# A fused attention and two-MLP kernel: other tiles for the second MLP's split activations and w_out sums, another DMA queue for weight stores, later result stores

## The chip, the cores and the metric

The kernel runs on one core of one Trainium2 chip. The metric is the device time of one execution in microseconds (us), median of several runs. The engines named here are TensorE (PE, with its weight loads PEld), VectorE (DVE), ScalarE (ACT), GpSimd (POOL) and SyncE (SP). SP computes nothing here: it issues DMAs, in order, one instruction after the other. ACT and POOL can issue DMAs too.

## The reference

Attention of 8 batches, 8 heads, 512 tokens and 32 state rows gives 4352 rows of 512. Two MLPs follow, each 512 to 2048 to 512 wide. Cut to what matters:

```python
x = attention(x, state)                     # 4352 x 512
h = x @ w_in                                # first MLP, 512 -> 2048
g = np.where(h >= 1, h, np.where(h <= -1, 0, (h + 1) ** 2 / 4))
x = g @ w_out                               # 2048 -> 512
h = x @ moe2_w_in                           # second MLP, 512 -> 2048
g = np.maximum(h, 0) + alpha * np.minimum(h, 0)
out = g @ moe2_w_out                        # 2048 -> 512, 4352 x 512
```

All inputs and outputs are fp32.

## The kernel before

**Precision.** Every fp32 operand of a product is split into a high and a low part (`hi_`, line 73, a cast on ACT; `lo_`, line 76, a subtraction on DVE, for some on POOL), and a product is three matmuls: high times high, high times low, low times high.

**Phases.** Up to about 730 us the kernel does attention and the first MLP. Beside them it prepares the second MLP's weights: sums of weight blocks, split into high and low, are stored to DRAM in `w1c` (from w_in) and `w2c` (from w_out) by `w_store` (line 681 on), and w_out in another order to `wod` by `w2o_store`. A part of the w2c sums is made in the first 50 or so items of the second MLP (`later` in `second`). In the first MLP POOL loads the split weights `ws` (line 489) from its own queue; these loads wait for nothing but their place in POOL's order and a free tile.

**The second MLP** (`second`, from about 728 us to the end) does both products by a Strassen form of seven products instead of eight. Tokens are worked on in five groups s = 0 to 4, of half-widths w = 512, 512, 384, 384, 384. There are 280 *h items* (`h_item`: one w_in product p of one block q, 6 matmuls of 128x128 by 128xw) and 280 *o items* (`o_item`: one quarter jj of a w_out product p, also 6 matmuls). An h item takes its weights from a tile `w1_qp` that `w1_get` loads (256 KB, SP); an o item takes them from `w2` tiles, where before one load of 512 KB serves two items (`w2_load`). The two kinds alternate: h item k+36 stands beside o item k.

After an h item its sum in PSUM goes through `h_after`: ACT copies it out or runs the slope, DVE adds on. For an o item, `o_prep` (three items ahead) makes the operand and splits it into `gh` (ACT) and `gl` (DVE). The products p = 0, 5, 6, 3 of the o items go one after the other into the same two PSUM tiles `oA`, and after each product (four items) `o_after` copies the state of the sum out: `c<-o`, by ACT on a group's first row r (line 836), by a DVE addition on its second (line 838). The next product of the chain adds on in the same PSUM tile, so its first matmul (`o<-gh`, line 824) has to wait for that copy.

On a group's second row the results are turned by DVE (`o_turn`, `ot`) for the products 3, 4, 2, 1 and stored by `ld.dma_start` in line 863: SP issues 64 KB DMAs, 16 or 12 in a row, twice for each group s.

**Tiles.** `U` gives one of 80 tiles of 2 KB a partition, `V` one of 11 of 4 KB. Before, w1, gh, gl, g, c and xh/xl are U tiles; w2 pairs, xr and ot are V tiles.

**Order.** The functions are called in program order; a list scheduler then goes through these instructions with modelled times and fixes the order on every engine and which slot a tile takes. On the chip each engine works in that order. A DMA that SP issues stands still until its destination tile is free, and everything behind it on SP with it.

In names such as `w1_213` the digits are q = 21 and p = 3; in `w2_450` r = 4, p = 5, jj = 0; `gh124` and `gs124` belong to o item 124; `c2110` is group 2, hh 1, tk 1, cc 0.

Of the kernel before, what the change touches and what calls it, by code (L numbers as in the profile page):

```python
# [9 lines left out]
F32 = mybir.dt.float32  # L10
F32R = mybir.dt.float32r
# [29 lines left out]
def kernel_body(ctx: ExitStack, tc: tile.TileContext, x, state, w1i, w1o, w2i, w2o, alpha, out):  # L41
# [52 lines left out]
    vd = [[dp.tile([NH, 128, 512], F32, name=f"vd{g}_{k}") for k in range(4)] for g in range(2)]  # L94
    xd = dp.tile([NO, 128, TOK], F32, name="xd")
    w1c = dp.tile([8, 7, 128, 512], F32, name="w1c")
    w2c = dp.tile([7, 4, 128, 1024], F32, name="w2c")
    wod = dp.tile([NF, 128, 512], F32, name="wod")
    wd = [dp.tile([2, DM, 512], F32, name=f"wd{k}") for k in range(4)]
    GRP = [1, 4]  # L100
# [581 lines left out]
    def w_store(key, *products):  # L682
        for p in products:
            t = WS.pop((key, p)).bitcast(F32)
            j = key[1]
            dst = w1c[j, p] if key[0] == "i" else w2c[p, j // 2, :, j % 2 * 512:(j % 2 + 1) * 512]
            ld.dma_start(out=dst, in_=t)

    def w2o_store(f):
        ld.dma_start(out=wod[f], in_=G.pop(("dec", ("w2o", f))))  # L690


    NSUP = len(HALF)

    BASE = [2 * sum(HALF[:s]) for s in (0, 1, 2, 4, 3)]
    C0 = [BASE[s // 2] + (s % 2) * HALF[s // 2] for s in range(2 * NSUP)]
    XR, XB, XT, HB, GB, GS, OA, OC, OT = {}, {}, {}, {}, {}, {}, {}, {}, {}

    def wof(s):
        return HALF[s]  # L700
# [42 lines left out]
            W1[q, p] = t  # L743

    def w2_load(m):
        if m < len(L2) and m % 2 == 0:
            r, p, jj = L2[m]
            t = V(f"w2_{r}{p}{jj}", F32R)
            ld.dma_start(out=t.bitcast(F32), in_=w2c[p, r % 2 * 2 + jj // 2])
            W2[m], W2[m + 1] = t[:, :512], t[:, 512:]  # L750

    def h_item(q, p):
        s = q // 8
# [38 lines left out]
    def o_prep(m):  # L792
        if m >= len(L2):
            return
        r, p, jj = L2[m]
        s = r // 2
        w, q = wof(s), 4 * r + jj
        b11, b21, b12, b22 = [GB[q, e, tk] for tk in range(2) for e in range(2)]
        src = {0: b11, 5: b11, 6: b12, 4: b11, 2: b22, 1: b21}.get(p)
        if p == 5:  # L800
            dve.tensor_tensor(out=b12, in0=b22, in1=b12, op=ALU.subtract)
            dve.tensor_tensor(out=b11, in0=b12, in1=b11, op=ALU.add)
        elif p == 3:
            src = U(f"t4{q}")[:, :w]
            dve.tensor_tensor(out=src, in0=b21, in1=b11, op=ALU.subtract)
        elif p == 4:
            dve.tensor_tensor(out=b11, in0=b22, in1=b11, op=ALU.subtract)
        h, l = U(f"gh{m}", F32R)[:, :w], U(f"gl{m}", F32R)[:, :w]
        hi_(h, src)
        lo_(l, src, h)  # L810
        GS[m] = (h, l)
# [17 lines left out]
    def o_after(r, p, cc, ps):  # L829
        s, last = r // 2, r % 2  # L830
        w = wof(s)
        hh, tk = {0: (0, 0), 5: (0, 1), 6: (1, 1), 3: (1, 0), 4: (1, 1), 2: (0, 1), 1: (0, 0)}[p]
        key = s, hh, tk, cc
        if p in A_CHAIN and not last:
            OC[key] = U(f"c{s}{hh}{tk}{cc}")[:, :w]
            act.copy(OC[key], ps)  # L836
        else:
            dve.tensor_tensor(out=OC[key], in0=ps, in1=OC[key], op=ALU.add)  # L838
        if last and p in (3, 4, 2, 1):
            o_turn(s, hh, tk, cc, OC.pop(key))  # L840

    def o_turn(s, hh, tk, cc, c):
        w, k = wof(s), 2 * hh + cc
        for v in range(0, w, 256):
            n = min(256, w - v)
            if (s, tk, v) not in OT:
                OT[s, tk, v] = [V(f"ot{s}{tk}{v}"), 0]
            o = OT[s, tk, v][0]
            dve.transpose(out=o[:, :4 * n].rearrange("p (j k x) -> p k j x", k=4, x=32)[:, k],
                          in_=c[:, v:v + n].rearrange("p (j t) -> p j t", t=32))  # L850
            OT[s, tk, v][1] += 1
            if OT[s, tk, v][1] < 4:
                continue
            del OT[s, tk, v]
            for u in range(0, n, 128):
                b, qq = divmod((C0[2 * s + tk] + v + u) // 128, 4)
                for i in range(4):
                    if b < NB:
                        dst = out[b * ROWS:b * ROWS + S, :].rearrange("(j t r) c -> t j r c", t=32, r=4)[:, :, qq]
                    else:  # L860
                        dst = out.rearrange("(b r) c -> r b c", r=ROWS)[S:, 4 * qq:4 * qq + 4]
                    eng = (ld, act)[i % 2] if s == NSUP - 1 else ld
                    eng.dma_start(out=dst[:, :, i * 128:(i + 1) * 128],
                                  in_=o[32 * i:32 * i + 32, 4 * u:4 * u + 512].rearrange("p (j c) -> p j c", j=4))

    def second():


        LAG = 36.5
        ev = [(n, 0, n) for n in range(len(L1))] + [(LAG + m, 1, m) for m in range(len(L2))]  # L870
# [8 lines left out]
        for _, kind, n in sorted(ev):  # L879
            if kind == 0:  # L880
                u, k, q, p = L1[n]
                h_item(q, p)
                h_after(q, p)
                w1_get(n + AW)
                todo = later.pop(n, [])
                s, j = divmod(u, 8)
                if j >= 6 and s + 1 < NSUP:
# [13 lines left out]
                run(*todo)  # L901
            else:
                if n == 0:
                    for m in range(6):
                        w2_load(m)
                    o_prep(0)
                    o_prep(1)
                    o_prep(2)
                w2_load(n + 6)
                o_prep(n + 3)  # L910
                o_item(n)


    side = defaultdict(list)
# [108 lines left out]
        at(gi(8, 2 + 2 * k), x_prep, 0, p)  # L1023
    for k, m in ((1, 3), (3, 2), (7, 4), (9, 1)):
        at(gi(8, k), x_sums, 0, m)
    AW = 7
    for k in range(AW):
        at(gi(8, 7 + k), w1_get, k)
    for j in range(2):
# [91 lines left out]
```

## Time and profile before

| what | value |
|---|---|
| median of 3 runs | 1438.97 us (1438.78 to 1440.12) |
| profiled execution, its own time | 1441.02 us |
| its span in the profile | 1439.1 us |
| PE busy | 1375.6 us, 96% of the span |
| DVE, ACT, POOL busy | 77%, 57%, 6% |
| DMA traffic | 320.62 MB, mean 223 GB/s |
| chain that ended last | PE 82%, DMA 9%, DVE 4%, ACT 2%, issue 2% |

The table is read so: an engine that is busy for 96% of the span leaves 63.5 us in which it did nothing; the waits and the timeline show where. A span is what the profiler saw from the first instruction to the last; the run's own time is 1.92 us longer. Matmul durations on PE overlap by their pipelining; an h or o item of 6 matmuls takes 1.36 us at w = 512 and 1.04 us at w = 384 at full clock (2.4 GHz; the other level is 1.2 GHz).

### The profile page before, as it was taken

The page shows a single profiled execution, that of the slowest core. Times are in us where ns is not written, and L with a number is a line of the kernel's source. Part 1 is how long each engine was busy: PE and PEld are TensorE (multiplying, and loading weights), DVE is VectorE, ACT ScalarE, POOL GpSimd, SP SyncE. Part 2 cuts the span into 40 slices and gives each one's busy share as a digit, 9 for nine tenths or more (in the row PEclk, how much of TensorE's full clock was granted, in tenths as well). Part 3 has the DMA queues.
Part 4 walks back from the last instruction along what each step waited for, and adds up shares of the span by engine and source line. Part 5 has one row for each costly group of instructions (what it writes and reads, how often), then busy time and mean ns, then how long its engine had stood idle before and what let it go on. Part 6 is the DMA issues. An engine that isn't in the chain of part 4 may idle for free.

```text
span 1439.1 us, 20152 instructions
## 1 busy us (share of the span) xinstructions
PE 1375.6 (96%) x6596; PEld 1168.0 (81%) x6596; DVE 1112.0 (77%) x2089; ACT 825.1 (57%) x1658; POOL 90.7 (6%) x94
## 2 busy tenths in 40 slices
PE   6799999999999999999999799999999899899997
PEld 4466688887787888888987678878888899799997
DVE  7888685868788997764858787868786877687687
ACT  5566676777776867664755464435444544364452
POOL 1000001111100000000200020001000100010000
PEclk9999999999999999999999999999999999999999
DMA  6898316788946543353859984676766876885773
GB/s 208 308 320 292 118 51 160 206 250 248 278 175 199 198 163 131 104 181 132 308 197 391 357 273 149 197 228 242 237 206 207 298 236 224 317 304 174 256 296 89
DMA packets 201111, 320.62 MB, mean 223 GB/s; under 512 B 53296, under 2 KB 82992, under 8 KB 201008
## 3 DMA queue, kind: packets, MB, share of 16 engines
q1 hardware_dynamic: 160288, 301.01, 61.4%
q0 software_dynamic: 33280, 8.51, 3.2%
q10 hardware_dynamic: 7440, 9.83, 2.0%
q8 instruction: 52, 0.85, 0.3%
q14 instruction: 51, 0.42, 0.1%
HBM read 242.10 MB, written 76.55 MB: 221 GB/s over the span
## 4 chain that ended last, share of the span: by engine, by line
PE 82%; DMA 9%; DVE 4%; ACT 2%; issue 2%; SPq 0%; ACTq 0%; POOL 0%; DVEq 0%; POOLq 0%
PE o L824 21%; PE accA L614 19%; PE ha L766 12%; PE hA L84 11%; PE hb L766 6%; PE accA L606 3%; PE hc L766 3%; DMA w<-w1c 2%; PE vgp L84 1%; DMA x<-in_x_dram 1%; DMA ws<-wd 1%; PE sc L84 1%; PE sr L84 1%; DMA vr<-vd 1%; DMA wr_wi<-in_moe_w_in_dram 1%
## 5 line engine op out<-in xcount | busy, mean ns | idle before, releaser
L824 PE MATMUL o<-gh,w 128*128 128x384 f32 (+1 forms) x1120 | 350.6, 363 | 19.4 <-ACT c L836 17.9
L76 DVE TENSOR_TENSOR gl<-g,gh 128x512 fp32r<-128x512 f32 (+2 forms) x368 | 234.3, 643 | 32.0 <-ACT gh L73 30.3
L824 PEld LDWEIGHTS o<-gh,w 128*128 128x128 f32 x1120 | 210.7, 191 | 39.6 <-ACT c L836 19.2
L73 ACT CAST gh<-g 128x512 fp32r<-128x512 f32 (+2 forms) x368 | 205.4, 565 | 36.2 <-DVE g L582 27.4
L824 PE MATMUL o<-gl,w 128*128 128x384 f32 (+1 forms) x560 | 203.0, 362 | 3.6 <-DVE gl L76 3.6
L766 PE MATMUL ha<-xh,w 128*128 128x384 f32 (+1 forms) x640 | 202.1, 358 | 1.0 <-ACT g L785 1.0
L773 ACT ACTIVATE m<-g 128x384 f32<-128x384 f32 (+1 forms) x120 | 68.3, 569 | 129.9 <-DVE g L789 127.9
L582 DVE SCALAR_TENSOR_TENSOR g<-y,hA 128x512 f32<-128x512 f32 (+1 forms) x144 | 93.9, 652 | 58.5 <-ACT y L580 58.0
L766 PEld LDWEIGHTS ha<-xh,w 128*128 128x128 f32 x640 | 119.4, 189 | 14.5 <-ACT g L785 3.5
L579 ACT ACTIVATE y<-hA 128x512 f32<-128x512 f32 (+1 forms) x144 | 82.5, 573 | 69.2 <-PE hA L84 67.5
L785 ACT COPY g<-ha 128x384 f32<-128x384 f32 (+1 forms) x120 | 62.9, 524 | 96.7 <-PE ha L766 93.8
L824 PEld LDWEIGHTS o<-gl,w 128*128 128x128 f32 x560 | 107.0, 191 | 12.6 <-DVE gl L76 5.0
L766 PE MATMUL ha<-xl,w 128*128 128x384 f32 (+1 forms) x320 | 114.2, 357 | 0.0
L766 PE MATMUL hb<-xh,w 128*128 128x384 f32 (+1 forms) x320 | 102.3, 360 | 6.2 <-DVE g L789 6.2
L789 DVE TENSOR_TENSOR g<-hb,g 128x384 f32<-128x384 f32 (+1 forms) x80 | 48.7, 609 | 66.9 <-PE hb L766 56.9
L774 DVE SCALAR_TENSOR_TENSOR g<-m,beta_sb,g 128x384 f32<-128x384 f32 (+1 forms) x120 | 81.4, 679 | 22.1 <-ACT m L773 20.8
L580 ACT ACTIVATE y<-y 128x512 f32<-128x512 f32 (+1 forms) x144 | 87.6, 608 | 4.4
L766 PEld LDWEIGHTS hb<-xh,w 128*128 128x128 f32 x320 | 59.5, 188 | 15.1 <-DVE g L789 9.4
L838 DVE TENSOR_TENSOR c<-o,c 128x384 f32<-128x384 f32 (+1 forms) x100 | 59.2, 605 | 12.3 <-PE o L824 11.8
L606 PE MATMUL accA<-g,wf_w1o 128*128 128x512 f32 x128 | 60.8, 607 | 4.6 <-DVE wf_w1o L399 4.6
L766 PEld LDWEIGHTS ha<-xl,w 128*128 128x128 f32 x320 | 60.3, 189 | 5.7
L494 ACT COPY vgo<-vgp 128x512 f32<-128x512 f32 x64 | 37.2, 585 | 41.7 <-PE vgp L84 22.0
(971 smaller groups left out, 3102.2 us busy)
## 6 DMA issues: line engine op xcount, KB each, us to landing
w<-w2c SPq DMA_DIRECT2D x140, 512.0 KB
w<-w1c SPq DMA_DIRECT2D x280, 256.0 KB
vd<-vgo SPq DMA_DIRECT2D x64, 256.0 KB
x<-in_x_dram SPq DMA_DIRECT2D x30, 512.0 KB
vr<-vd SPq DMA_DIRECT2D x56, 256.0 KB
w1c<-wsi SPq DMA_DIRECT2D x56, 256.0 KB
w2c<-wso SPq DMA_DIRECT2D x56, 256.0 KB
wr_wi<-in_moe_w_in_dram SPq DMA_DIRECT2D x16, 512.0 KB
```

Of the source, the lines that this page charges most:

```text
L73: act.copy(h, raw)
L76: (eng or dve).tensor_tensor(out=l, in0=raw, in1=h.bitcast(F32), op=ALU.subtract)
L84: pe.matmul(ps, a, b, start=(k == 0), stop=(k == n - 1))
L579: act.activation(out=y[:, :n], in_=ps, func=AF.Relu, bias=0.5, scale=0.5)
L580: act.activation(out=y[:, :n], in_=y[:, :n], func=AF.Square)
L582: dve.scalar_tensor_tensor(out=g[:, :n], in0=y[:, :n], scalar=1.0, in1=ps, op0=ALU.min, op1=ALU.max)
L606: pe.matmul(ACC[k], w[:, k * 128:(k + 1) * 128], g, start=(f == 0), stop=(f == NF - 1))
L614: pe.matmul(ACC[k][:, :n], a, b, start=(f == 0 and j == 0), stop=(f == NF - 1 and j == 2))
L766: pe.matmul(ps, a[:, kk], b, start=(first and m == 0), stop=(m == 5), skip_group_check=True)
L773: act.activation(out=m, in_=h, func=AF.Relu, scale=-1.0)
L774: dve.scalar_tensor_tensor(out=g, in0=m, scalar=beta_sb[:, f:f + 1], in1=h, op0=ALU.mult, op1=ALU.add)
L824: pe.matmul(ps, a, b, start=(p in (0, 4, 1) and jj == 0 and k == 0), stop=(jj == 3 and k == 2), skip_group_check=True)
```

## The change

Six things are changed in the second MLP and its preparation.

- `w2c` is laid out in single quarters, and each o item has its own load of 256 KB into a U tile, five items ahead, instead of 512 KB for two into a V tile, six ahead.
- The split operand of an o item is one V tile `gs` (high in the first half, low in the second) instead of two U tiles.
- `w_store` and `w2o_store` (128 DMAs) are issued by POOL instead of SP.
- The result stores are taken out of `o_turn` and issued by `o_store` after the o item that follows the one that completed them.
- On a group's second row product 3 is no longer turned on its own but together with product 1, except in the last group.
- w1 loads run 7 items ahead up to item 36 and 5 ahead from 37 on, instead of 7 throughout.

```diff
--- before.py
+++ after.py
@@ -94,7 +94,7 @@
     vd = [[dp.tile([NH, 128, 512], F32, name=f"vd{g}_{k}") for k in range(4)] for g in range(2)]
     xd = dp.tile([NO, 128, TOK], F32, name="xd")
     w1c = dp.tile([8, 7, 128, 512], F32, name="w1c")
-    w2c = dp.tile([7, 4, 128, 1024], F32, name="w2c")
+    w2c = dp.tile([7, 8, 128, 512], F32, name="w2c")
     wod = dp.tile([NF, 128, 512], F32, name="wod")
     wd = [dp.tile([2, DM, 512], F32, name=f"wd{k}") for k in range(4)]
     GRP = [1, 4]
@@ -683,18 +683,17 @@
         for p in products:
             t = WS.pop((key, p)).bitcast(F32)
             j = key[1]
-            dst = w1c[j, p] if key[0] == "i" else w2c[p, j // 2, :, j % 2 * 512:(j % 2 + 1) * 512]
-            ld.dma_start(out=dst, in_=t)
+            pool.dma_start(out=w1c[j, p] if key[0] == "i" else w2c[p, j], in_=t)
 
     def w2o_store(f):
-        ld.dma_start(out=wod[f], in_=G.pop(("dec", ("w2o", f))))
+        pool.dma_start(out=wod[f], in_=G.pop(("dec", ("w2o", f))))
 
 
     NSUP = len(HALF)
 
     BASE = [2 * sum(HALF[:s]) for s in (0, 1, 2, 4, 3)]
     C0 = [BASE[s // 2] + (s % 2) * HALF[s // 2] for s in range(2 * NSUP)]
-    XR, XB, XT, HB, GB, GS, OA, OC, OT = {}, {}, {}, {}, {}, {}, {}, {}, {}
+    XR, XB, XT, HB, GB, GS, OA, OC, OT, DONE = {}, {}, {}, {}, {}, {}, {}, {}, {}, []
 
     def wof(s):
         return HALF[s]
@@ -743,11 +742,10 @@
             W1[q, p] = t
 
     def w2_load(m):
-        if m < len(L2) and m % 2 == 0:
+        if m < len(L2):
             r, p, jj = L2[m]
-            t = V(f"w2_{r}{p}{jj}", F32R)
-            ld.dma_start(out=t.bitcast(F32), in_=w2c[p, r % 2 * 2 + jj // 2])
-            W2[m], W2[m + 1] = t[:, :512], t[:, 512:]
+            W2[m] = U(f"w2_{r}{p}{jj}", F32R)
+            ld.dma_start(out=W2[m].bitcast(F32), in_=w2c[p, r % 2 * 4 + jj])
 
     def h_item(q, p):
         s = q // 8
@@ -805,7 +803,8 @@
             dve.tensor_tensor(out=src, in0=b21, in1=b11, op=ALU.subtract)
         elif p == 4:
             dve.tensor_tensor(out=b11, in0=b22, in1=b11, op=ALU.subtract)
-        h, l = U(f"gh{m}", F32R)[:, :w], U(f"gl{m}", F32R)[:, :w]
+        v = V(f"gs{m}", F32R)
+        h, l = v[:, :w], v[:, 512:512 + w]
         hi_(h, src)
         lo_(l, src, h)
         GS[m] = (h, l)
@@ -836,7 +835,9 @@
             act.copy(OC[key], ps)
         else:
             dve.tensor_tensor(out=OC[key], in0=ps, in1=OC[key], op=ALU.add)
-        if last and p in (3, 4, 2, 1):
+        if last and (p in (4, 2, 1) or p == 3 and s == NSUP - 1):
+            if p == 1 and s < NSUP - 1:
+                o_turn(s, 1, 0, cc, OC.pop((s, 1, 0, cc)))
             o_turn(s, hh, tk, cc, OC.pop(key))
 
     def o_turn(s, hh, tk, cc, c):
@@ -852,6 +853,15 @@
             if OT[s, tk, v][1] < 4:
                 continue
             del OT[s, tk, v]
+            DONE.append([2, s, tk, v, n, o])
+
+    def o_store(late):
+        for d in list(DONE):
+            d[0] -= 1
+            if d[0] and not late:
+                continue
+            DONE.remove(d)
+            _, s, tk, v, n, o = d
             for u in range(0, n, 128):
                 b, qq = divmod((C0[2 * s + tk] + v + u) // 128, 4)
                 for i in range(4):
@@ -864,7 +874,6 @@
                                   in_=o[32 * i:32 * i + 32, 4 * u:4 * u + 512].rearrange("p (j c) -> p j c", j=4))
 
     def second():
-
 
         LAG = 36.5
         ev = [(n, 0, n) for n in range(len(L1))] + [(LAG + m, 1, m) for m in range(len(L2))]
@@ -881,7 +890,9 @@
                 u, k, q, p = L1[n]
                 h_item(q, p)
                 h_after(q, p)
-                w1_get(n + AW)
+                while NEXT[0] <= n + (AW if n < 37 else 5):
+                    w1_get(NEXT[0])
+                    NEXT[0] += 1
                 todo = later.pop(n, [])
                 s, j = divmod(u, 8)
                 if j >= 6 and s + 1 < NSUP:
@@ -901,14 +912,15 @@
                 run(*todo)
             else:
                 if n == 0:
-                    for m in range(6):
+                    for m in range(5):
                         w2_load(m)
                     o_prep(0)
                     o_prep(1)
                     o_prep(2)
-                w2_load(n + 6)
+                w2_load(n + 5)
                 o_prep(n + 3)
                 o_item(n)
+                o_store(n == len(L2) - 1)
 
 
     side = defaultdict(list)
@@ -1023,7 +1035,7 @@
         at(gi(8, 2 + 2 * k), x_prep, 0, p)
     for k, m in ((1, 3), (3, 2), (7, 4), (9, 1)):
         at(gi(8, k), x_sums, 0, m)
-    AW = 7
+    AW, NEXT = 7, [7]
     for k in range(AW):
         at(gi(8, 7 + k), w1_get, k)
     for j in range(2):
```

Since tiles and program order change, the scheduler gives other orders. Three places follow, all near the passage from group s = 1 to s = 2 or inside it.

ACT around the copies c2110 and c2111 that follow product p = 6 of row r = 4 (group 2), before; `m` is the slope, `gh` a split, `g` a copy of an h item, `c` the copy of the chain's sum:

```order
L773 ACTIVATE m221_11543<-ha22_11381 128x384
L73 CAST gh124_11550<-t416_11548 128x384
L785 COPY g2300_11567<-ha23_11560 128x384
L73 CAST gh125_11579<-t417_11577 128x384
L773 ACTIVATE m221_11597<-g2211_11493 128x384
L73 CAST gh126_11608<-t418_11606 128x384
L836 COPY c2110_11615<-o400_11322 128x384
L836 COPY c2111_11620<-o401_11326 128x384
```

and of the changed kernel:

```order
L771 ACTIVATE m221_11539<-ha22_11377 128x384
L783 COPY g2300_11564<-ha23_11557 128x384
L73 CAST gs124_11548<-t416_11546 128x384
L73 CAST gs125_11576<-t417_11574 128x384
L771 ACTIVATE m221_11593<-g2211_11489 128x384
L835 COPY c2110_11612<-o400_11302 128x384
L835 COPY c2111_11617<-o401_11306 128x384
L73 CAST gs126_11606<-t418_11604 128x384
```

The two copies stood behind the cast gh126 of an operand t418 that DVE has to make first; now that cast (gs126) stands behind the copies. In front of the copies there remains m221, whose operand g2211 DVE adds up from an h item.

DVE at the same place, before, from g2200 (a sum that waits for the h item hc22) to t418 and the split behind it:

```order
L76 TENSOR_TENSOR gl124_11551<-t416_11548,gh124_11550 128x384
L789 TENSOR_TENSOR g2200_11388<-hc22_11708,g2200_11388 128x384
L716 TENSOR_TENSOR xt330_11571<-xr311_11392,xr301_11423 128x384
L716 TENSOR_TENSOR xt331_11573<-xr311_11392,xr301_11423 128x384
L805 TENSOR_TENSOR t417_11577<-g1710_10637,g1700_10495 128x384
L807 TENSOR_TENSOR g1700_10495<-g1711_10588,g1700_10495 128x384
L76 TENSOR_TENSOR gl125_11580<-t417_11577,gh125_11579 128x384
L716 TENSOR_TENSOR xt320_11602<-xt330_11571,xr300_11473 128x384
L774 SCALAR_TENSOR_TENSOR g2211_11493<-m221_11597,beta_sb_78,g2211_11493 128x384
L716 TENSOR_TENSOR xt321_11604<-xt331_11573,xr300_11473 128x384
L805 TENSOR_TENSOR t418_11606<-g1810_10806,g1800_10664 128x384
L807 TENSOR_TENSOR g1800_10664<-g1811_10759,g1800_10664 128x384
```

and of the changed kernel:

```order
L803 TENSOR_TENSOR t416_11546<-g1610_10458,g1600_10294 128x384
L805 TENSOR_TENSOR g1600_10294<-g1611_10405,g1600_10294 128x384
L715 TENSOR_TENSOR xt330_11568<-xr311_11388,xr301_11420 128x384
L76 TENSOR_TENSOR gs124_11548<-t416_11546,gs124_11548 128x384
L715 TENSOR_TENSOR xt331_11570<-xr311_11388,xr301_11420 128x384
L803 TENSOR_TENSOR t417_11574<-g1710_10634,g1700_10492 128x384
L787 TENSOR_TENSOR g2211_11489<-hb22_11585,g2211_11489 128x384
L805 TENSOR_TENSOR g1700_10492<-g1711_10585,g1700_10492 128x384
L76 TENSOR_TENSOR gs125_11576<-t417_11574,gs125_11576 128x384
L772 SCALAR_TENSOR_TENSOR g2211_11489<-m221_11593,beta_sb_78,g2211_11489 128x384
L715 TENSOR_TENSOR xt320_11598<-xt330_11568,xr300_11470 128x384
L715 TENSOR_TENSOR xt321_11600<-xt331_11570,xr300_11470 128x384
```

Before, g2200 from hc22 stands ahead of nine others, t417 and t418 among them. Now t418 follows the last row shown, and g2200 comes after it. On TensorE the two h items of blocks 22 and 23 that stood between the last item of p = 6 and the first of p = 3 (q 22 p 1, and q 23 p 5) are three now (q 23 p 5, q 22 p 2, q 22 p 1); at the passage in group 0 there are three instead of one.

SP at the end of group 1, before: `out_0_dram<-ot` are the result stores, the others loads of weights:

```order
L749 DMA w2_452_11316<-w2c_90 128x1024
L742 DMA w1_220_11201<-w1c_89 128x512
L863 DMA out_0_dram<-ot110_11069 32x4x128 x8
L863 DMA out_0_dram<-ot11256_11071 32x4x128 x8
L742 DMA w1_214_11228<-w1c_89 128x512
L742 DMA w1_225_11248<-w1c_89 128x512
L742 DMA w1_212_11272<-w1c_89 128x512
L863 DMA out_0_dram<-ot100_10968 32x4x128 x8
L863 DMA out_0_dram<-ot10256_10970 32x4x128 x8
L742 DMA w1_226_11314<-w1c_89 128x512
L742 DMA w1_211_11341<-w1c_89 128x512
```

and of the changed kernel:

```order
L873 DMA out_0_dram<-ot11256_11062 32x4x128 x8
L741 DMA w1_213_11218<-w1c_89 128x512
L748 DMA w2_402_11220<-w2c_90 128x512
L741 DMA w1_220_11239<-w1c_89 128x512
L748 DMA w2_403_11241<-w2c_90 128x512
L741 DMA w1_214_11262<-w1c_89 128x512
L748 DMA w2_450_11264<-w2c_90 128x512
L741 DMA w1_225_11295<-w1c_89 128x512
L748 DMA w2_451_11297<-w2c_90 128x512
L873 DMA out_0_dram<-ot100_11273 32x4x128 x8
L873 DMA out_0_dram<-ot10256_11275 32x4x128 x8
L741 DMA w1_212_11337<-w1c_89 128x512
```

Between the two series of result stores there stood three w1 loads; now there are eight loads, and the w1 load that follows the second series is w1_212 instead of w1_226.

## Rows read from the trace of the kernel before

**Rows 1.** Windows: span, busy us (instructions) of PE, PEld, DVE, ACT, POOL; PEclk, DMA share, GB/s
```profile
0.00:730.00 730.00, 704.70 (x3240) 562.33 (x3241) 561.40 (x1062) 493.07 (x959) 56.80 (x66) 1.00 0.62 200
730.00:1439.10 709.10, 670.87 (x3358) 605.66 (x3356) 550.57 (x1028) 332.03 (x699) 33.95 (x28) 0.98 0.72 246
```

**Rows 2.** Waits of PE in 730:1439.1: who waited for whom: us in total, times, longest
```profile
PE o L824 <- ACT c L836: 17.9, 3, 7.6
PE hb L766 <- DVE g L789: 6.2, 8, 0.9
PE o L824 <- DVE gl L76: 3.6, 4, 1.2
```

**Rows 3.** Timeline of PE, then DVE, then ACT: start, us, instruction [idle before <-releaser]
```profile
1130.54 0.69 PE L824 MATMUL o<-gh,w 128*128 128x384 f32 x1 [5.11 <-ACT c L836]
...
1124.42 0.56 DVE L789 TENSOR_TENSOR g<-hc,g 128x384 f32<-128x384 f32 x1 [1.51 <-PE hc L766]
...
1128.96 0.55 DVE L805 TENSOR_TENSOR t<-g,g 128x384 f32<-128x384 f32 x1
...
1126.89 0.52 ACT L773 ACTIVATE m<-g 128x384 f32<-128x384 f32 x1
1129.60 0.51 ACT L73 CAST gh<-t 128x384 fp32r<-128x384 f32 x1 [2.19 <-DVE t L805]
1130.02 0.85 ACT L836 COPY c<-o 128x384 f32<-128x384 f32 x2
```

**Rows 4.** Chain of waits after two of these gaps: start, us, piece
```profile
828.54 5.49 PE o L824 x12
...
835.58 2.74 PE o L824 x12
...
1130.54 4.21 PE o L824 x12
...
1135.82 2.08 PE o L824 x12
```

**Rows 5.** Windows behind the first gap and around 1105 us, columns as in rows 1
```profile
830.00:832.00 2.00, 2.00 (x6) 1.61 (x5) 1.99 (x3) 1.41 (x4) 1.37 (x1) 0.50 0.60 240
...
1103.00:1107.00 4.00, 2.97 (x9) 2.46 (x10) 4.00 (x10) 1.78 (x4) 0.00 (x0) 0.61 0.77 219
```

**Rows 6.** Timeline of SP at the end of group 1
```profile
1085.00 7.79 SPq L863 DMA_DIRECT2D out_dram<-ot  x16
1092.90 1.38 SPq L742 DMA_DIRECT2D w<-w1c  x3
1094.38 7.77 SPq L863 DMA_DIRECT2D out_dram<-ot  x16
1102.25 0.89 SPq L742 DMA_DIRECT2D w<-w1c  x2
```

**Rows 7.** Timeline of PE behind these loads
```profile
1105.78 0.69 PE L766 MATMUL hc<-xh,w 128*128 128x384 f32 x1 [0.41 <-DMA w<-w1c]
```

**Rows 8.** Chain of waits: the h item that follows p = 1's last o item, and a load
```profile
1092.12 1.04 PE hc L766 x6
...
1104.17 6.58 DMA w<-w1c
...
1220.29 1.04 PE o L824 x6
```

**Rows 9.** Timeline of SP at the ends of group 2 and group 0
```profile
1215.44 5.69 SPq L863 DMA_DIRECT2D out_dram<-ot  x12
...
1224.00 5.72 SPq L863 DMA_DIRECT2D out_dram<-ot  x12
...
939.17 8.40 SPq L863 DMA_DIRECT2D out_dram<-ot  x16
```

**Rows 10.** The loads ws of line 489: their landing, one landing in the chain, PE's wait
```profile
DMA to landing us min/median/max: 8.4/11.6/22.7
...
310.70 18.09 DMA ws<-wd
...
PE vgp L510 <- DMA ws<-wd: 2.6, 1, 2.6
```

**Rows 11.** Waits of SP over the whole span
```profile
SPq L749 <- PE o L824: 129.2, 42, 8.9
...
SPq L687 <- DVE wsi L76: 68.9, 39, 9.3
```

## The prediction, made before the changed kernel ran

> **What bounds the kernel now.** I first read the windows of the two halves. Up to 730 us PE is busy for 704.7 us, in the second MLP for 670.9 of 709.1 us [rows 1]: an edit can win there only what PE stands idle (38.2 us) or does at a low clock. In the first half little is idle after the start. DMA share is 0.72 in the second MLP, so transfers have room on average, and a late one is late by its place in a queue. Next I read PE's waits of the second MLP [rows 2]. They name 17.9 us in only three waits of an o item for the copy `c` by ACT, 6.2 us in eight waits for DVE's `g`, and 3.6 us in four waits for DVE's `gl`; about 7.6 us are the kernel's tail, where the last results leave.
>
> Then the timeline around one of the three large gaps shows why it is there [rows 3]. PE waits 5.11 us until 1130.54 for copies that ACT starts at 1130.02. The values to copy had long been ready, but in front of the copies ACT has the cast gh126, which waits for t418 on DVE. DVE reaches t418 at 1128.96 only, since it waited 1.51 us until 1124.42 for an h item (g2200 from hc22) and then did nine others. The row order on ACT and DVE that does this was shown with the change. The other two large gaps have the same cause: 7.65 us at group 0's passage and 5.11 at group 3's make up the 17.9.
>
> A gap costs more than itself. In the chain, the twelve matmuls after the gap at 828.54 take 5.49 us, and twelve such a little later 2.74; at 1130.54 it is 4.21 against 2.08 [rows 4]. The window there has a granted clock of 0.50, that is 1.2 GHz, after PE stood still [rows 5]. So 2.8 and 2.1 us are lost behind the gap, and 2.1 at the third by the same sizes.
>
> **What the change takes away.**
> - *The three gaps.* The copies now stand ahead of gs126 on ACT, and g2200 stands behind t418 on DVE. PE has three h items (3.1 us) between the last of p = 6 and the first of p = 3, where it had two, and 4.1 us at group 0 with one before. The copies wait for m221 alone. So 17.9 us go, and with them 2.8 + 2.1 + 2.1 = 7.0 us of low clock.
> - *The gl waits.* A gap of this kind lies at the end of each of the groups 0 to 3: the subtraction stood on DVE behind a sum that waits for PE. It now stands well ahead of it: −3.6 us. With the one at 1103.6 goes a stretch of lower clock: 2.97 us of PE work at 0.61 [rows 5], worth 2.97 × 0.39 = 1.2 us. The eight waits for `g` (6.2 us) stay: the order that makes them is unchanged.
>
> Together 17.9 + 7.0 + 3.6 + 1.2 = 29.7 us.
>
> **What the change costs.**
> - *The result stores.* A series of 16 stores holds SP for 7.8 us [rows 6], and only what SP issued ahead of it feeds PE meanwhile. Before, w1 ran 7 items ahead and w2, in its own tiles, further still; three w1 loads lay between the two series. PE just missed one load then: hc at 1105.78 waited 0.41 us for a load whose issue began about 0.45 us into the pair at 1102.25 [rows 6, 7], that is 3.0 us earlier. Now both run 5 items ahead, and eight loads lie between the series (8 × 0.445 = 3.6 us by the pair's 0.89). With the first series where it was, at 1085.00, the second ends at 1085.00 + 7.79 + 3.6 + 7.77 = 1104.2, and the load w1_212 behind it lands 3.0 later, at 1107.2. PE wants it nine items after product 1's last o item, which ended at 1092.12 [rows 8]; nine items of 1.04 and one `g` wait of 0.72 make 1102.2. PE stands 5.0 us. At group 2 the series take 5.69 and 5.72 [rows 9]: 1215.44 + 5.69 + 3.6 + 5.72 + 3.0 = 1233.4, wanted at 1220.29 + 1.04 [rows 8] + 9 × 1.04 + 0.72 = 1231.4: 2.0 us. Group 3 is like group 2. At group 0 the series is 8.40 [rows 9], but nine items take 9 × 1.36 us: also 2.0. The last group has no load behind its stores. Sum 11.0 us, and 2.1 of low clock behind the longest: +13.1 us.
>  The landing is the unknown: 3.0 us is the row right behind a series of stores; a load in the chain of waits took 6.58 us from there on [rows 8]. From below the stall is nothing, if SP reaches the first series earlier. I take 3.0, since the same kind of place gives it, and keep both ends.
> - *Twice as many w2 loads.* 140 more issues of about 0.44 us are 62 us of SP's time in a stage in which SP waits 129.2 us for w2 tiles alone [rows 11]; 128 stores leave SP. I take nothing. If SP had no such slack, it would show as more of the stall above, priced there.
>  The Trainium skill speaks against small transfers (DMA: Bandwidth & Descriptors, section "Measured (HBM→SBUF, 128 partitions, SWDGE, issued from GpSimd)": batch to 1 MiB or more); its fit in "Anatomy of one DMA" gives, as an estimate, 2.6 us for 256 KB and 3.2 for 512 KB. If each DMA's time stood alone, the second MLP's 280 + 140 loads would need 1176 us, which the 709.1 us at a share of 0.72 [rows 1] contradict; so here they overlap and the split costs engines' time only in part. By the fit unoverlapped the sum would rise by 280 us, and I don't use it.
> - *POOL's stores.* SP waited 68.9 us in 39 waits, up to 9.3, for the values of w1c's stores [rows 11]; POOL does so now, and behind it stand the ws loads and the halves of xl. Of the ws loads one landed after 18.09 us and made PE wait 2.6; so it was issued 15.5 ahead of its use, and the median of 11.6 has 3.9 to spare. I take nothing. The ends are −2.6 (that wait goes, as another order moves it) and +7.2 for a load that lands at the longest, 22.7 [rows 10]. The w2c stores of the second MLP are issued at least 12 pairs of items ahead of their loads by the code, 33 us at 2 × 1.36 a pair, more than the longest landing here.
> - *`gs` in V, turning of product 3.* The cast and the subtraction stay the same instructions on other tiles; the turns stay as many, and those of product 3 now lie beside product 1's. That can delay the second series by their time, while the o items run on: I take nothing, and the bounds of the landing hold it too.
>
> **Sum.** 1441.0 − 29.7 + 13.1 = 1424.4 us by the profiled execution, which is 2.05 above the median: **1422.4 us**.
>
> **The rivals.**
> - *A, the stores don't block* (17%). SP is ahead enough, or stalls hide behind the `g` waits. For it: PE missed only 0.41 us so far [rows 7]. Against it: the look-ahead is shorter by two items and the stores have five loads more between them. 1441.0 − 29.7 − 2.05 = 1409.3 us.
> - *B, slower: loads behind the stores land late* (13%). All eight loads held back are issued at once behind the second series, and land at 6.58 [rows 8] rather than 3.0: +3.6 at each of four ends, 11.0 + 14.4 = 25.4 us, and each stall now brings the low clock, 2.8 + 3 × 2.1 = 9.1. That is 34.5 against 29.7 won: 1441.0 + 4.8 − 2.05 = 1443.8 us. It decides from about 7.4 us per end on. Against it: the 3.0 was measured behind such a series, at a share of 0.77 [rows 5].
> - *C, the copies are still late* (13%). On DVE six instructions of 0.55 stand ahead of g2211's sum, if none is done early; sum 0.56, m221 0.52 and half of the 0.85 of the copies [rows 3] make 4.8 us from the h item's end. PE has four items, 4.2 us. A wait of 0.6 to 1.5 us with 2.1 of low clock would remain at three places: about +10, 1432 us.
> - *D, slower: ws loads starve on POOL* (5%). Three loads at 22.7 us are 21.6 us of PE's time, more than the 16.6 left of the gain: 1444 us. Between them lie 42 stores. Against it: 32 loads had one wait in all.
>  The Trainium skill adds a reason (SBUF — State Buffer, section "SBUF: two separate sides"): descriptors of a DMA on POOL's queue are written by GpSimd, which a DVE operation in its two-port mode keeps out. Here POOL's loads land at 8.4 to 22.7 us [rows 10], SP's at 3.0 to 6.6; no run shows whether DVE is why.
>
> **How the numbers follow.** Forecast 52%, A 17, C 13, B 13, D 5. The forecast's own range is 1414 (only group 1 stalls, −6, and a little of the `g` waits) to 1431 (each stall with its low clock, +7). The range reaches over A and C: 1406 to 1441, leaving out most of B and D and a little of A. About 0.2%, 2.9 us, is what a measurement of this kernel tells from no change. Faster: 50 of the forecast, 17 of A, 9 of C: 0.76. Same: 2 + 3 of C, 4 of B, 1 of D: 0.10. Slower: 0.14.
>
> **What would show it.** PE's waits for `c` should be gone or under 1 us each, those for `gl` too, and windows near 830, 1130 and 1257 us should show a clock of 1.00. At the ends of groups 0 to 3 an h item should wait for `w<-w1c`, 2, 5, 2 and 2 us, each behind a second series of stores on SP. Waits for `ws` should stay within one or two. I am wrong if a `c` wait is left above 2 us, if `w<-w1c` or `w<-w2c` waits come to over 25 us or to none, or if the first 730 us change by more than 5.

## The result: slower, and where the time went

The changed kernel takes 1448.36 us, median of four runs (1446.45 to 1449.92), against 1439.21 for the kernel before (1438.78 to 1440.12): ratio 1.0062, 95% interval 1.0045 to 1.0080. The forecast was 1422.4, with a range up to 1441. The profiled execution took 1446.45 us, 5.4 more than that of before.

The two windows of the changed kernel, columns as in [rows 1]:

```profile
0.00:730.00 730.00, 703.82 (x3220) 560.77 (x3221) 563.98 (x1060) 493.12 (x958) 101.43 (x152) 0.99 0.62 199
730.00:1444.40 714.40, 676.13 (x3378) 609.81 (x3376) 553.80 (x1029) 335.94 (x700) 69.64 (x71) 0.98 0.74 245
```

PE's idle time in the second MLP is what it was (38.3 us after, 38.2 before), but it is made of other waits. The waits of PE there (who for whom: us in total, times, longest):

```profile
PE hb L764 <- DMA w<-w1c: 17.4, 4, 6.1
PE ha L764 <- ACT g L783: 5.8, 7, 1.3
PE o L823 <- DVE gs L76: 2.2, 1, 2.2
PE hb L764 <- DVE g L787: 1.9, 2, 1.1
PE o L823 <- ACT gs L73: 1.0, 3, 0.6
PE o L823 <- DVE c L837: 0.9, 1, 0.9
```

The three waits for ACT's copy `c` (17.9 us [rows 2]) are gone entirely, as forecast. In their place stand four waits of an h item for its weights, one at the end of each of the groups 0 to 3. The timeline of PE shows them:

```profile
961.13 0.47 PE L764 MATMUL hb<-xh,w 128*128 128x512 f32 x1 [4.11 <-DMA w<-w1c]
...
1109.89 0.66 PE L764 MATMUL hb<-xh,w 128*128 128x384 f32 x1 [6.05 <-DMA w<-w1c]
...
1236.64 0.66 PE L764 MATMUL hb<-xh,w 128*128 128x384 f32 x1 [4.32 <-DMA w<-w1c]
...
1363.09 0.42 PE L764 MATMUL hb<-xh,w 128*128 128x384 f32 x1 [2.92 <-DMA w<-w1c]
```

What held the load back at 1109.89 stands in the timeline of SP, the answer to [rows 6]:

```profile
1086.36 7.66 SPq L873 DMA_DIRECT2D out_dram<-ot  x16
1094.12 0.39 SPq L741 DMA_DIRECT2D w<-w1c  x1
...
1097.46 0.38 SPq L748 DMA_DIRECT2D w<-w2c  x1
1097.93 8.99 SPq L873 DMA_DIRECT2D out_dram<-ot  x16
1107.02 0.40 SPq L741 DMA_DIRECT2D w<-w1c  x1
```

The load that PE waits for is issued at 1107.02, straight behind the second series, and lands 2.74 us later by the chain of waits. Between the series lie the eight loads of the order. SP's own waits in 1070 to 1104 us tell two more things:

```profile
SPq L873 <- DVE ot L850: 8.6, 1, 8.6
...
SPq L873 <- DMA w<-w1c: 1.2, 3, 0.5
SPq L873 <- DMA w<-w2c: 1.0, 3, 0.4
```

SP reaches the first series 8.6 us before there is anything to store and stands there, with all later loads behind it; and inside the second series it waits 2.2 us for loads just issued (the third to the eighth store of the series each for the landing of the load eight DMAs before it), which is why that series takes 8.99 us and not 7.77. At all four places the load that PE waits for lands 2.74 to 2.86 us after its issue.

Each of the four stalls brings the low clock. The window behind the second, columns as above:

```profile
1110.00:1112.00 2.00, 2.00 (x7) 2.00 (x8) 0.00 (x0) 0.00 (x0) 0.00 (x0) 0.50 0.87 288
```

Summed over windows of 1 us as PE's busy time times the missing part of the clock, the low clock costs 10.1 us in the second MLP (8.4 before): 1.7, 2.6, 2.4 and 1.7 behind the four stalls, and 1.7 at 835 us behind a wait for `gs`. That wait of 2.23 us is new: at the passage from the first to the second row of group 0, DVE is busy for all of 825 to 835 us and ACT for 9.24 of the 10, and PE is there before its operand. Two of DVE's instructions there are longer than their like, beside a subtraction that POOL does:

```profile
827.41 3.98 POOL L76 TENSOR_TENSOR xl<-xr,xh 128x512 fp32r<-128x512 f32 x1 [1.89 <-ACT xh L73]
...
829.56 0.68 DVE L76 TENSOR_TENSOR gs<-t,gs 128x512 fp32r<-128x512 f32 x1
830.16 1.78 DVE L772 SCALAR_TENSOR_TENSOR g<-m,beta_sb,g 128x512 f32<-128x512 f32 x1
831.87 1.89 DVE L76 TENSOR_TENSOR xl<-xt,xh 128x512 fp32r<-128x512 f32 x1
```

They take 1.78 and 1.89 us, where the median in the second MLP is 0.75 for the first kind and 0.68 for the second: 2.2 us more, as long as the wait. That POOL's subtraction is what holds them up no run tests.

### The profile page after: what moved, and what is told of

Read it like the earlier page. It is cut to its first block, busy times and chain, and to the rows that moved or that the text cites. A ratio compares the mean times of both kernels' runs of the same rounds, so it can differ in the third digit from the quotient of the medians.

```text
span 1444.4 us, 20642 instructions
## 1 busy us (share of the span) xinstructions
PE 1380.0 (96%) x6596; PEld 1170.6 (81%) x6596; DVE 1117.8 (77%) x2089; ACT 829.1 (57%) x1658; POOL 171.1 (12%) x222
## 4 chain that ended last, share of the span: by engine, by line
PE 74%; DVE 10%; DMA 8%; issue 3%; ACT 2%; SPq 2%; POOL 0%; DVEq 0%; ACTq 0%; POOLq 0%
PE accA L614 19%; PE o L823 17%; PE hA L84 11%; PE ha L764 11%; PE hb L764 5%; PE hc L764 3%; PE accA L606 3%; DMA w<-w1c 2%; DMA ws<-wd 2%; DVE gs L76 2%; SPq L873 1%; PE sr L84 1%; PE vgp L84 1%; PE sc L84 1%; DVE g L772 1%
## 5 line engine op out<-in xcount | busy, mean ns | idle before, releaser
L823 PE MATMUL o<-gs,w 128*128 128x384 f32 (+1 forms) x1680 | 369.6, 360 | 4.7 <-DVE gs L76 2.2
L823 PEld LDWEIGHTS o<-gs,w 128*128 128x128 f32 x1680 | 305.5, 190 | 32.5 <-DVE gs L76 3.2
L764 PE MATMUL ha<-xh,w 128*128 128x384 f32 (+1 forms) x640 | 205.1, 365 | 5.9 <-ACT g L783 5.8
L73 ACT CAST gs<-g 128x384 fp32r<-128x384 f32 (+1 forms) x240 | 124.8, 554 | 71.7 <-PE o L823 35.8
L76 DVE TENSOR_TENSOR gs<-g,gs 128x384 fp32r<-128x384 f32 (+1 forms) x240 | 142.5, 629 | 7.8 <-ACT gs L73 7.6
L764 PE MATMUL hb<-xh,w 128*128 128x384 f32 (+1 forms) x320 | 103.7, 361 | 19.5 <-DMA w<-w1c 17.4
L76 DVE TENSOR_TENSOR gl<-g,gh 128x512 fp32r<-128x512 f32 (+1 forms) x128 | 92.0, 719 | 25.0 <-ACT gh L73 23.4
L772 DVE SCALAR_TENSOR_TENSOR g<-m,beta_sb,g 128x384 f32<-128x384 f32 (+1 forms) x120 | 84.7, 706 | 19.4 <-ACT m L771 18.6
L73 ACT CAST gh<-g 128x512 fp32r<-128x512 f32 (+1 forms) x128 | 75.7, 591 | 32.1 <-DVE g L582 30.2
L76 POOL TENSOR_TENSOR xl<-xr,xh 128x384 fp32r<-128x384 f32 (+1 forms) x15 | 24.1, 1606 | 374.1 <-DVE gs L76 208.5
```

What stands on the lines that cost most here:

```text
L73: act.copy(h, raw)
L76: (eng or dve).tensor_tensor(out=l, in0=raw, in1=h.bitcast(F32), op=ALU.subtract)
L764: pe.matmul(ps, a[:, kk], b, start=(first and m == 0), stop=(m == 5), skip_group_check=True)
L772: dve.scalar_tensor_tensor(out=g, in0=m, scalar=beta_sb[:, f:f + 1], in1=h, op0=ALU.mult, op1=ALU.add)
L823: pe.matmul(ps, a, b, start=(p in (0, 4, 1) and jj == 0 and k == 0), stop=(jj == 3 and k == 2), skip_group_check=True)
```

## The experiments

Theory 1: SP stands in two series of stores at each group's end; the w1 load behind the second comes too late. Theory 2, formed on the way: one edit alone (gs) carries the order's gain, and the shorter look-aheads take it back. "Waits for weights" are PE's for w1c and w2c in the second MLP. The median of the kernel before was 1441.3 us beside e1 to e4, 1440.8 beside e5 to e8, 1439.9 beside e9 to e12 and 1441.4 beside e13; ratios are to that.

| run | edit | us | ratio (95%) | waits for weights |
|---|---|---|---|---|
| e1 | change, stores on POOL | 1416.8 | 0.984 (0.982 to 0.986) | 0.4 |
| e2 | change, weight stores on SP | 1449.5 | 1.006 (1.004 to 1.008) | 20.2 |
| e3 | change, w1 7 ahead | 1438.5 | 0.998 (0.996 to 0.999) | 15.6 |
| e4 | change, stores at once | 1450.6 | 1.007 (1.005 to 1.009) | 23.0 |
| e5 | before, stores on POOL | 1423.5 | 0.988 (0.985 to 0.990) | 1.8 |
| e6 | before, gs | 1449.4 | 1.005 (1.003 to 1.008) | 8.8 |
| e7 | before, gs, stores on POOL | 1413.5 | 0.981 (0.978 to 0.984) | 0 |
| e8 | before, gs, w2 in U | 1441.1 | 1.000 (0.999 to 1.002) | 17.5 |
| e9 | change, w1 9 and w2 8 ahead | 1436.7 | 0.998 (0.996 to 0.999) | 17.1 |
| e10 | change, half the stores on POOL | 1421.8 | 0.988 (0.986 to 0.989) | 1.3 |
| e11 | change, group 1's stores on POOL | 1438.2 | 0.999 (0.998 to 1.000) | 13.0 |
| e12 | change, stores on POOL, w1 7 ahead | 1416.3 | 0.984 (0.983 to 0.986) | 0 |
| e13 | change, stores two per o item | 1430.5 | 0.993 (0.991 to 0.995) | 4.2 |

**e1, result stores on POOL.**

```diff
-                    eng = (ld, act)[i % 2] if s == NSUP - 1 else ld
+                    eng = (ld, act)[i % 2] if s == NSUP - 1 else pool
```

> The changed kernel with one edit: the result stores of groups 0 to 3 are issued by POOL instead of SP; nothing else moves on PE around the passages. Theory 1 (SP stands in the two series of stores, and the weight loads behind them come late): the four waits of an h item for w<-w1c (17.4 us) and the 8.4 us of low clock behind them go, so 1448.4 - 25.8 = about 1423 us. Rival (the loads are late since twice as many w2 loads and the stores fill the DMA engines, whoever issues): waits for w1c or w2c stay above 10 us, 1440 us or more.

Measured 1416.8 us, 31.5 below the changed kernel and 6 below theory 1's sum (of which 3.3 lie in the first half, which ends that much earlier in this execution). The waits of PE in its second MLP:

```profile
PE o L823 <- DVE c L837: 4.5, 4, 2.2
PE ha L764 <- ACT g L783: 3.0, 4, 1.1
PE o L823 <- DVE gs L76: 2.2, 1, 2.2
PE hb L764 <- DVE g L787: 1.9, 2, 1.1
PE o L823 <- ACT gs L73: 0.6, 1, 0.6
PE o L823 <- DMA w<-w1c: 0.4, 1, 0.4
```

The same bytes go through the same 16 engines, and the loads are in time: theory 1 holds, the rival falls. Low clock is left at one place, 1.7 us. One thing the expectation had wrong: with the stores gone from SP the planner also moves h items on PE (after o item 115 it gives one to each o item, and q 21 p 2, which stalled, comes two o items later). This run alone does not part SP's time from that order; e4 and e10 do.

**e2, weight stores back on SP** (`pool.dma_start` to `ld.dma_start` in `w_store` and `w2o_store`).

> The changed kernel with the weight stores (w1c, w2c, wod) back on SP. Theory (POOL's stores ahead of its ws loads made the first 730 us longer by the 3.5 us that the trace shows, the second MLP has nothing of it): about 1445 us, and the last matmul of the first MLP about 3 us earlier than in the changed kernel. Rival (the first half's difference is chance between executions, or comes from the start): 1447 to 1450 us with the waits for ws still there.

1449.5 us: no gain, so POOL's stores are not what made the first half longer. The first MLP's last matmul begins at 733.4 us here, at 732.7 in the changed kernel, at 729.9 before; but with the same weight stores on POOL at 728.5 in e9 and e10, and with them on SP at 732.1 in e7. It moves by up to 5 us between executions whatever the queue; why, these runs don't settle.

**e3, w1 seven ahead throughout.**

```diff
-                while NEXT[0] <= n + (AW if n < 37 else 5):
+                while NEXT[0] <= n + AW:
```

> The changed kernel with w1 loads 7 items ahead throughout, instead of 5 from item 37 on. Theory 1: behind the second series stands the load of an h item that comes one or two items later, so each of the four waits is 1 to 2 us shorter; 1448.4 - 4 to 8 = 1440 to 1444 us, the wait is then for w1_x1 or for a w2 tile, which is still only 5 ahead. Rival (look-ahead alone made the stalls): the waits go, about 1423 us.

1438.5 us, 10 below the changed kernel, a little more than theory 1 said, and the place is as said: hc, product 1, waits now (15.6 us in four waits) and not hb. But the waits did not each become 1 to 2 us shorter: they are 1.9, 6.0, 5.0 and 2.7 us, 1.8 less in all. Most of the gain is elsewhere: the low clock costs 4.9 us instead of 10.1, and the waits for ACT's `g` fell from 5.8 to 1.2. The rival falls, since the waits did not go.

**e4, stores at once** (`o_store(n == len(L2) - 1)` to `o_store(True)`).

> The changed kernel with the result stores issued at once, not after the next o item. Theory 1: six loads instead of eight lie between the two series, but w1_212 then stands two loads further behind, so it lands at the same time: 1447 to 1449 us, no change. Rival (the delay of the stores is what makes the loads late): the waits shrink by more than half, 1435 us or less.

1450.6 us, 1.6 above the range given but within 2.2 of the changed kernel: the delay by an item is not the cause, as theory 1 said. PE's order is that of the changed kernel, item by item, and the waits for weights are longer (23.0 us), not shorter.

**e5 and e7, the kernel before, and with gs, with the stores on POOL; e6, gs alone.** e5 is e1's line put into the kernel before; e6 is

```diff
-        h, l = U(f"gh{m}", F32R)[:, :w], U(f"gl{m}", F32R)[:, :w]
+        v = V(f"gs{m}", F32R)
+        h, l = v[:, :w], v[:, 512:512 + w]
```

> The kernel before with one edit: the result stores of groups 0 to 3 are issued by POOL. Theory 1 (the series on SP hurts only with the changed kernel's short look-ahead): the three waits for c stay, only the 0.4 us wait for w1c goes: 1439 to 1441 us, no change. Rival (the stores on SP cost as much in the kernel before too, hidden in the other waits): 1430 us or less.

> The kernel before with one edit of the change: gh and gl in one V tile gs. Its order has the copies ahead of the cast at the three passages, three or more h items in front of them, and keeps both look-aheads, with four loads between the two series of stores. Theory 2 (gs alone brings the order's gain, and w2's and w1's shorter look-ahead take it back): the waits for c and gl and their low clock go, 29.7 us, w1c waits stay under 2 us an end: 1441.3 - 29.7 + 0 to 4 = 1411 to 1416 us. Rival (the V tiles, now shared by w2 pairs, gs, xr and ot, run out and SP or ACT wait for them; or the gain needs the other edits): 1425 us or more.

> The kernel before with gs in one V tile and the result stores of groups 0 to 3 issued by POOL. Theory 2: with 7 items of look-ahead the series on SP cost at most the few us that gs alone still has there, so this is 0 to 4 us below gs alone: 1410 to 1413 us. Rival (the loads behind the series are what is left in gs alone): 10 us or more below gs alone.

e5 is 17 us faster than before, where theory 1 expected nothing. e5's waits for `c` and `g`:

```profile
PE o L824 <- ACT c L836: 9.8, 3, 7.6
PE hb L766 <- DVE g L789: 2.4, 3, 0.9
PE o L824 <- DVE gl L76: 1.5, 2, 0.8
```

Of the three large gaps one is left whole (7.6), one is 1.9 and one 0.3. Its order says how: between the last item of p = 6 and the first of p = 3 at group 2 it has three h items (q 23 p 5, q 22 p 2, q 22 p 1), as the changed kernel has, where the kernel before has two. The same holds at group 3. Only the queue of the stores was edited, so it is the scheduler, presumably since it no longer sees SP held, that places the h items in another way. The large gaps of before were thus in part the stores' doing, by way of the plan.

gs alone (e6) brings the order of the copies, and `c` falls from 17.9 to 2.7. But it loses:

```profile
PE o L825 <- DVE gs L76: 11.6, 9, 1.8
PE hc L766 <- DMA w<-w1c: 8.6, 3, 4.2
PE hb L766 <- DVE g L789: 6.2, 8, 0.9
PE o L825 <- ACT c L837: 2.7, 1, 2.7
```

At the old look-ahead, 8.8 us of waits for weights (the line above and one wait of 0.2) and nine waits for gs are there: theory 2's first half is wrong, 1449.4 us where it said 1411 to 1416. With the stores on POOL beside it (e7) both fall (gs to 3.8, weights to none), and e7, 36 us below e6 as the rival there said, has the lowest median of all, 1413.5, though its interval overlaps those of e1 and e12. The rival named for e6, V tiles that run out, is seen in the waits: in the second MLP ACT's splits `gs` wait 87.0 us for o items, which free those tiles, and SP's w2 loads 308.0 (before, the splits wait 0.2 so, and SP's w2 loads 129.2). But e7 has 72.1 and 355.9 us of the same and is fast, so these waits alone do not make e6 slow. What separates a slow kernel of this set from a fast one is in both cases the series on SP.

**e8, gs and w2 in U tiles, w1 7 ahead.**

> The kernel before with gs and w2's 256 KB loads into U tiles, five items ahead; w1 7 ahead, weight stores on SP, results stored at once. Theory 2: against gs alone it has w2's short look-ahead and eight loads in the place of the four: the w1c or w2c waits at the four ends are back at 12 to 16 us with their low clock, 1434 to 1440 us, as in the changed kernel with w1 7 ahead (1438.5). Rival (w1's look-ahead alone makes the stalls): 1412 to 1418 us.

1441.1 us with 17.5 us of waits for weights. It lies a little above its range. The waits for weights are back, as theory 2 said (8.8 in e6), but the time is not: against e6 at 1449.4 it is faster, with 3.1 us of waits for gs instead of 11.6 and none for ACT's `c`. Theory 2's second half holds for the waits and not for the time; since gs and w2 share V tiles in e6 and not here, the look-ahead's own price is not parted from that.

**e9, look-ahead 9 and 8.**

```diff
-                while NEXT[0] <= n + (AW if n < 37 else 5):
+                while NEXT[0] <= n + (AW if n < 37 else 9):
-                w2_load(n + 5)
+                w2_load(n + 8)
```

> The changed kernel with w1 loads 9 and w2 loads 8 items ahead (5 and 5 there), stores still on SP. Theory 1 (the stall is look-ahead that is shorter than two series and what lies between): four pairs of items more, over 8 us at 2.08 a pair, cover stalls of 2.9 to 6.1, so the w1c waits fall under 2 us an end: 1420 to 1428 us. Rival (loads stand behind tiles that come free late, or the engines are full): waits of 2 us or more at each end, 1434 us or more.

1436.7 us, and 17.1 us of waits for weights: the forecast of 1420 to 1428 is missed, and the longer look-ahead does not cover the series. The timeline of SP and then of PE:

```profile
1081.60 7.65 SPq L873 DMA_DIRECT2D out_dram<-ot  x16
...
1093.16 10.66 SPq L873 DMA_DIRECT2D out_dram<-ot  x16
1103.92 0.37 SPq L741 DMA_DIRECT2D w<-w1c  x1
...
1107.05 0.98 PE L764 MATMUL ha<-xh,w 128*128 128x384 f32 x2 [5.41 <-DMA w<-w1c]
```

It is again the first load behind the second series, now w1_230, that PE wants. In e9's order PE takes six h items in a row after o item 115 (q 21 p 4, 6, 3, 2, 1 and q 23 p 0); in the changed kernel q 23 p 0 comes four o items later. So here the plan spends the look-ahead by drawing h items forward. Of the rival's reasons little shows: between the series SP's eight loads wait for no tile beyond 0.3 us, and the load behind lands 2.99 us after its issue; inside the second series SP waits 2.1 us for loads to land.

**e10 and e11, part of the stores on POOL:** every second store (`else (ld, pool)[i % 2]`), and group 1's alone (`else pool if s == 1 else ld`).

> The changed kernel with every second result store of groups 0 to 3 on POOL, the others on SP. Theory 1: each series holds SP half as long, 2 x 3.9 us less before the load that PE wants (2 x 2.9 in groups 2 and 3), which is more than the stalls of 4.1, 6.1, 4.3 and 2.9: waits for w1c gone or under 1 us, 1417 to 1422 us, as with all of them on POOL. Rival (the DMA engines' load counts, not SP's time): w1c waits at half of the 17.4, 1432 us.

> The changed kernel with the result stores of group 1 alone on POOL. Theory 1: only that end's wait of 6.1 us and its 2.6 of low clock go, the other three stay: 1448.4 - 8.7 = about 1440 us. Rival (the ends hang together, and a stall that goes at one is met again at the next): 1445 us or more, with longer waits at groups 2 and 3.

e10: 1421.8 us with 1.3 us of waits for weights. e11: 1438.2 us; the ends of groups 0, 2 and 3 keep their waits and group 1's is gone:

```profile
961.15 0.77 PE L764 MATMUL hb<-xh,w 128*128 128x512 f32 x1 [4.73 <-DMA w<-w1c]
...
1231.52 0.66 PE L764 MATMUL hb<-xh,w 128*128 128x384 f32 x1 [4.71 <-DMA w<-w1c]
...
1358.06 0.42 PE L764 MATMUL hb<-xh,w 128*128 128x384 f32 x1 [3.00 <-DMA w<-w1c]
```

The dose follows theory 1 in both. e10 is also the cleanest of the runs: at the ends of groups 1 to 3 PE's order differs from the changed kernel's only in the products 6 and 3 of one block, which stand one or two o items earlier; the item that stalled (product 2) and its neighbours keep their places, and all but 1.3 us of the stalls goes with SP's time.

**e12, stores on POOL and w1 7 ahead.**

> The changed kernel with the result stores of groups 0 to 3 on POOL and w1 loads 7 items ahead throughout. Theory 1: with no series on SP five items are enough, so the longer look-ahead brings nothing: 1415 to 1419 us, as with the stores alone on POOL (1416.8). Rival (part of the look-ahead's loss has nothing to do with the stores): 1412 us or less.

1416.3 us, the same as e1: without the series, five items are enough.

**e13, stores on SP, two after each o item.** `o_store` puts the DMAs of a finished tile in a list instead of issuing them, and then:

```diff
+        for k in range(2):
+            if PEND and PEND[0][0] < NSUP - 1:
+                s, eng, d, i = PEND.pop(0)
+                eng.dma_start(out=d, in_=i)
```

> The changed kernel with the result stores still on SP, but two after each o item instead of a series of 16 or 12 at once. SP's time for them is the same. Theory 1 in its narrow form (a series in one piece on SP is what makes the loads late; two loads of 0.47 us and two stores of 0.49 are 1.9 us, less than the 2.08 or 2.74 us of a pair of items): w1c waits gone or under 1 us, 1417 to 1423 us. Rival (SP's time as a whole is short near the ends, so any order of the same DMAs on SP stalls): w1c or w2c waits of 8 us or more in total, 1432 us or more.

1430.5 us: the waits for weights fall from 17.4 to 4.2, the time by 18 us. SP issues the same DMAs, and the engines carry as many packets from 733 us on (108189, 107359 in the changed kernel, 95480 in e1), so the engines' load is not what stalls PE; the stores' standing in one piece costs most, though here too the plan moves h items. The forecast of 1417 to 1423 was too low: 4.2 us of weight waits are left, the largest 2.45 at 1119 us, and about 15 of other small ones (e1: 0.4 and 13).

## Why the prediction was wrong

- **What goes away: right in its main part.** The three gaps of 17.9 us and their low clock are gone, and so are the `gl` waits. (At group 0 the passage had two h items before, hc and ha from 818.0 to 820.7 us, not one.) What stands in their place was not in the sum: waits for ACT's `g` (5.8 us against 1.0 before) and one for `gs` (2.2, and 1.7 of low clock, which the same wait does not bring in e1, e4 and e11), and 0.9 for a copy by DVE; the waits for `g` by DVE, taken to stay, fell from 6.2 to 1.9. Together 4.8 + 2.2 + 1.7 + 0.9 - 4.3 = 5.3 us more than forecast.
- **The step that failed most: "The result stores", mis-sized.** Mechanism, place and load were as said. The term was 11.0 us of stalls and 2.1 of low clock, 13.1; measured are 17.4 and 8.4, 25.8. At group 1 the first series began at 1086.36, not 1085.00, the eight loads took 3.8 us, not 3.6, the second series 8.99, not 7.77, and the landing 2.74, not 3.0: the load lands 2.6 us later than forecast, and PE wanted it 1.6 later (1103.84): 6.05 for 5.0. At groups 0 and 2 it was 4.1 and 4.3 for 2.0, at group 3 2.9; at group 2 the series took 6.75 and 6.42 us, not 5.69 and 5.72. What the prediction had no term for is that a series stands for the landing of the loads in front of it. And the low clock came behind all four, not only behind the longest. The prediction gave no reason for that limit, though on its other side it had priced low clock behind waits of under 1 us (1.2 us near 1103.6).
- **POOL's stores: right.** The ws loads on POOL cost PE 3.9 us in two waits, as against 2.6 [rows 10], and e2 shows no loss by the queue. In the profiled execution the first half nevertheless ends 2.8 us later.
- **The split of w2's loads: no cost seen.** e1 has all 280 w2 loads of 256 KB and no wait of PE for them but one of 0.4 us, an o item's. The Trainium skill's rule to batch to 1 MiB ("DMA: Bandwidth & Descriptors", section "Measured (HBM→SBUF, 128 partitions, SWDGE, issued from GpSimd)") is stated for DMAs that GpSimd issues, where these are SP's; it did not decide here.
- **The sum.** By the profiled executions: forecast -16.6, plus 12.7 for the stores, 5.3 for the other waits and 2.8 in the first half, is +4.2; measured +5.4. The medians are 9.2 apart: the profiled execution of the changed kernel is the fastest of its four, that of before is above its median. That scatter is not explained.
- **The rivals.** B named the right place, and that each stall brings the low clock; its price (1443.8) was the nearest but for D's 1444. Its mechanism was not the one: the loads behind the series landed 2.74 to 2.86 us after their issue, not 6.58. It was SP that issued them late. B had 13%; the chance of a stall price between forecast and B was put too low, for the bound of the landing was weighed, and not that several terms in the row could each be a little worse at once. A and C fall: the stores do block, and no wait for ACT's `c` is left. D's ws loads cost 3.9 us, and 27 stores lie between them, not 42.
- **The signs of being wrong.** None of the three came: no `c` wait by ACT, 17.4 us of weight waits (the bound was 25), 2.8 us in the first half (the bound was 5). Bounds that, met together, allow a time outside the range could not warn.

## What to carry to other kernels

A queue that issues loads in order should not issue bursts that wait for results: SP stood 8.6 us before a series and 29 us from its last load ahead of it to the first load behind both, while PE goes on for only as long as the loads ahead reach. Count that stretch from the last load before the burst to the landing of the first behind it, against the items that PE has in hand; and move the burst to another queue or spread it before lengthening the look-ahead, since a scheduler may spend the look-ahead on drawing work forward. If the order comes from a planner, an edit on one queue can move a gap on another engine: e5 changed nothing but the stores' queue, and of three gaps two shrank from 5.1 to 0.3 and 1.9 us.

## What was not expected of the hardware

DMAs that POOL issues in place of SP did not hold the others up: POOL issued the stores of 64 KB at about 0.54 us each, against SP's 0.48, and PE's waits for weights fell from 17.4 to 0.4 us at a DMA share of 0.77 in the second MLP (0.74 with them on SP).

```profile
730.00:1414.60 684.60, 663.51 (x3359) 601.20 (x3357) 551.12 (x1027) 338.52 (x699) 127.93 (x182) 0.99 0.77 256
...
1083.35 5.40 POOL L873 DMA_DIRECT2D out_dram<-ot  x10 [1.92 <-issue]
```

The rows are e1's: its second MLP among the windows, and one piece of POOL's timeline. In the second MLP of all these runs, every wait of PE of 2.9 us or more was followed by 1.5 to 3.0 us of loss at the clock of 1.2 GHz; the changed kernel's four stalls cost about half as much again. Shorter waits are not so regular: that of about 2.2 us for `gs` in group 0 was followed by 1.7 us of loss in the changed kernel and in e10, and by none in e1, e4 and e11; one of 2.66 us at 828 us in e7 by none, one of 1.89 at 1238 us in e5 by 1.7.
